# Threshold attention and a bilinear layer on one core: shorter reads of the turned weights, a changed front, stores by halves

## The chip, the core and the metric

The kernel runs on one core of a Trainium2 chip. The core has a matrix engine (PE, with its weight loads shown apart as PEld), a vector engine (DVE), a scalar engine (ACT), a general engine (POOL) and an engine that issues transfers (SP); 16 DMA engines move the data. Matrix products are written to PSUM, a small memory of banks; all else lies in SBUF, which has 128 partitions. The metric is the device time of the whole kernel in microseconds, as the median of several runs. One further execution is profiled, and all durations below are of that execution.

## The reference

```python
scores = (q @ k.T) / 8                          # 8 batches, 8 heads, 576 x 64 each
thresh = max(scores, axis=-1) - tau
scores = where(scores >= thresh, scores, -1e9)
attn = exp(scores - max(scores)); attn /= sum(attn) + 1e-9
x = (attn @ v) as (4608, 512)                   # heads side by side
out = ((x @ w_a) * (x @ w_b)) @ w_out           # 512 -> 1536 -> 512
```

q, k and v are 32-bit floats; the three weight matrices come as 64-bit floats and are turned into 32-bit ones on the chip.

## The kernel before

**Tiling.** Two heads make a pair, 32 pairs in all. The queries of a pair are cut into units of 128 (u = 0 to 3); the last 64 queries of two neighbouring pairs make a fifth unit (u = NT = 4). The list `units` gives their order: for the first four pairs first u = 0 and 1 of all of them, then the rest. The main loop (L1117) goes over slots g; slot g computes the scores of unit g and, woven in between, later stages of earlier units and parts of the second layer.

**A unit's way.** `scores` (L389) multiplies q and k on PE into two PSUM tiles, one a head. DVE takes the row maxima `mx` (L411) and subtracts the threshold's width to get `thr` (L412). `weigh` (L422): ACT scales the maximum to `bias` (L431) and takes Exp (L432) into `tw`; DVE multiplies it by the mask (L435) and sums. The weights are then turned. Up to unit 8 this is PE's work (`turn_pe`, L472: products with a diagonal of reciprocals). From unit 8 on, DVE transposes blocks of 32 x 32 (L502), four transfers of 144 KB write them to a scratch in DRAM (`swap<-tw`), and `turn_back` (L517) reads them back the other way round (`wT<-swap`), in two transfers of 288 KB. `product` (L538) multiplies them with v into `pv`. Two buffers `wT` stand for the two units of a product, so the reads of the next two units wait until a product is done.

**The weight matrices.** 36 pieces of 128 x 512. Each is loaded by SP (L271), split by ACT (L298 and L299), clamped by POOL (L305), given its sign by DVE (`convert_sign`, L311), shifted by DVE (`convert_shift`, L319) and added by POOL (`convert_add`, L324). The table `early` gives two pieces to each of the slots 0 to 3 and 10 to 14, and three to each of the slots 4 to 9; ACT's half is done in slot g and the rest, by `convert_rest(g, k)` for piece k, in slot g + 1. While that goes on (`state["wide"]`, slots 0 to 15), scores use 128 query columns a product. `advance` emits parts of the second layer on PE.

**The first four pairs.** `load_rows` (L193) loads all of q and k in rows, and PE transposes them (`prep_pe`, L368, by 96 rows at a time); DVE copies q out of PSUM (L383), ACT copies k. For all later pairs q and k come by `load` in blocks of 32 x 32 and are transposed by DVE (`prep`, L361, with the transposition at L365): q in two parts, `q0` (256 queries) and `q1` (320 queries), in two buffers that all pairs share.

**Order and pace.** Each engine works through its instructions in the order in which the program writes them (`keep_order`). Transfers go to SP's queue. Up to slot 36 `post` (L139) issues them where they are posted; after that (`state["paced"]`) they go into the list `bulk`, from which `pump` (L152) takes them one entry at a time. Each entry makes SP wait for the PE instruction that was last at that place; an entry of n elements is charged 320 x n / 36864 columns of PE's work (`passed`, L169) before the next is taken. Eight semaphores serve the transfers in turn: each transfer waits for the one eight before it.

**The second layer.** `ffn` works in blocks of 256 rows; its finished rows go to `pending` (`rows_out`, L1001), and `store` (L1011) posts them one slot later, 128 x 512 at a time (64 rows for the tail blocks).

Of the kernel before, what the change touches and what calls it, by code (L numbers as in the profile page):

```python
# [10 lines left out]
FP32 = mybir.dt.float32  # L11
# [43 lines left out]
def kernel(  # L55
# [38 lines left out]
    nc = tc.nc  # L94
    B, H, S, D = q.shape
    P = 128
# [3 lines left out]
    HP = H // 2  # L100
# [5 lines left out]
    R = 96  # L106
    NR = S // R
    SH = S // 2
# [84 lines left out]
    def load_rows(i, name, room, engine=nc.sync):  # L193

        b, hp = pairs[i]
        for j in range(2):
            rows = {"q": q, "k": k}[name][b, 2 * hp + j]
            engine.dma_start(room[:, :, j * D:(j + 1) * D], rows.rearrange("(n p) d -> p n d", p=R))
        loaded.setdefault(i, {})[name] = room

    def load_v(i, again=False):
# [106 lines left out]
    def convert_sign(n):  # L308
        if n in stages:
            low, hi = stages[n].bitcast(U32), raws.pop(n)[:, :, 1]  # L310
            nc.vector.scalar_tensor_tensor(out=low, in0=hi, scalar=0x80000000, in1=low,  # L311
                                           op0=ALU.bitwise_and, op1=ALU.bitwise_or)
            if n in taken:
                extra.append(taken.pop(n))

    def convert_shift(n):
        if n in stages:
            top = pieces[n][0].bitcast(U32)
            nc.vector.tensor_scalar(top, top, 3, None, op0=ALU.logical_shift_left)  # L319

    def convert_add(n):
        if n in stages:
            top, low = pieces[n][0].bitcast(I32), stages.pop(n).bitcast(I32)
            nc.gpsimd.tensor_tensor(top, top, low, op=ALU.add)  # L324
            state["added"] += 1
# [42 lines left out]
    def prep_pe(i, name):  # L368

        m = loaded[i][name]  # L370
        if name == "q":
            mT = first_sb[:, i * S:(i + 1) * S]
        else:
            mT = work.tile([P, S], FP32, tag="kT", bufs=HP, name="kT")
        tp = banks(SH, "tp")
        for c in range(2):
            for n in range(NR // 2):
                nc.tensor.transpose(tp[:, c, n * R:(n + 1) * R], m[:, c * (NR // 2) + n], ident[0:R, 0:R])
        prepared.setdefault(i, {})[name] = mT
        return mT, tp  # L380

    def prep_copy(mT, tp):
        nc.vector.tensor_copy(mT.rearrange("p (c k) -> p c k", c=2), tp)  # L383

    def columns():

        return P if state["wide"] else D

    def scores(i, u):  # L389
        qT, kT = prepared[i]["q" if i < HP else "q1" if u > 1 else "q0"], prepared[i]["k"]  # L390
        base = HALF if i >= HP and u > 1 else 0
        sc = [banks(SH, "sc") for _ in range(2)]
        wide = D if u == NT else columns()
        each = [(c, t, j) for c in range(2) for t in range(2 if wide == D else 1) for j in range(2)]
        if units.index((i, u)) < BY_HEAD:
            each.sort(key=lambda x: x[2])
        for c, t, j in each:
            r = slice(j * D, (j + 1) * D)
            if u < NT:
                m, o, q0 = j, t, u * P + t * D - base  # L400
            else:
                m, o, q0 = t, j ^ t, MAIN - base
                qT, kT = prepared[i + t]["q" if i < HP else "q1"], prepared[i + t]["k"]
            nc.tensor.matmul(sc[m][o * D:o * D + wide, c], qT[r, q0:q0 + wide],  # L404
                             kT[r, c * SH:(c + 1) * SH], start=True, stop=True)
        mx = small.tile([P, 2], FP32, tag="mx", name="mx")
        thr = small.tile([P, 2], FP32, tag="thr", name="thr")
        bias = small.tile([P, 2], FP32, tag="bias", name="bias")
        for j in range(2):
            c = slice(j, j + 1)  # L410
            nc.vector.tensor_reduce(mx[:, c], sc[j], axis=AX.XY, op=ALU.max)  # L411
        nc.vector.tensor_scalar(thr, mx, cut, None, op0=ALU.subtract)  # L412
        scored[i, u] = (sc, thr, bias, mx)
# [103 lines left out]
    def turn_back(i, u):  # L517

        key = "wT", i, min(u // 2, 1) if i >= HP else u // 2
        if u < NT or i < HP:  # L520
            flush(("tw", i, u))
            swap = swaps.pop((i, u)).rearrange("g p e -> p g e")
            turned[i, u] = turned_tile((i, u))
            for y in range(0, G, 2):
                post(key, (turned[i, u][:, y:y + 2].rearrange("p g s e -> p g (s e)"), swap[:, y:y + 2]))
        if i >= HP and u == (3 if i % 2 else NT):
            flush(("tw", i - i % 2, NT))
            swap = swaps[i - i % 2, NT].rearrange("g p e -> p g e")
# [482 lines left out]
    def store(n):  # L1011

        for _ in range(n):
            post("out", pending.pop(0))

    BLOCK_COLS = NF * 2 * HP * HALF + 2 * NF * DM

# [84 lines left out]
    nc.vector.tensor_tensor(cut, cut, big, op=ALU.add)  # L1102
    early = {}

    def convert_rest(g, k):

        for n in early.get(g - 1, [])[k:k + 1]:
            convert_sign(n)
            convert_shift(n)
            convert_add(n)  # L1110

    n = 0
    for g in range(NPIECES):
# [3 lines left out]
    for g in range(len(units) + PV_LAG):  # L1117
# [26 lines left out]
            running["owed"] -= NSLOT * P // 2  # L1144
        if g < 3:
            prep_copy(*prep_pe(g + 1, "q"))
        convert_rest(g, 0)
        if g == 0:
            for c in range(0, 2 * QUARTER - 2 * CW + 1, 2 * CW):
                extra.append(more_u32[:, c:c + 2 * CW].rearrange("p (f w) -> p f w", w=2))  # L1150
# [7 lines left out]
        load_weights(RAWS if g < 9 else 3, most=1)  # L1158
        if here:
            weigh(i, u)  # L1160
        for p in range(HP, NPR):
            for name, d in (("q0", 1), ("q1", 1)):
                if g == (second if name == "q1" else first)[p] - d - (name == "q1" and p % 2):
                    prep(p, name)
        if here and g < BY_PE:
# [33 lines left out]
        elif here:  # L1199
            reciprocal(i, u, nc.scalar if converting else nc.vector)  # L1200
            normalise(i, u)
        convert_rest(g, 1)
        if g <= BY_PE:
            advance(pace)
        convert_rest(g, 2)
        for n in early.get(g, [])[1:]:
            convert_first(n)
            convert_clamp(n)
        load_weights(RAWS if g < 9 else 3, most=1)
        for p in range(HP, NPR):  # L1210
            for name, d in (("q0", 3), ("k", 4), ("q1", 3)):
                if g == (second if name == "q1" else first)[p] - d - (name == "q1" and p % 2):
                    load(p, name)
        for p in range(1, NPR):
# [67 lines left out]
```

## Time and profile before

| | us |
|---|---|
| median of 3 runs | 1406.4 (1405.77, 1406.4, 1414.82) |
| the profiled execution | 1400.57 |
| its span | 1398.8 |
| PE busy | 1361.5 |
| DVE busy | 1013.9 |
| ACT busy | 680.8 |
| POOL busy | 492.8 |
| mean granted clock of PE | 0.998 of full speed |

The span runs from the first to the last instruction of the profiled execution; the 1.8 us that its time has more lie around it. The row of an instruction group tells when it starts, how long it lasts, on which engine and line, what it writes and reads, and in brackets how long its engine stood idle before it and what ended that. An instruction that is held up inside the engine, not by a semaphore, shows a longer duration instead.

### The profile page before, as it was taken

To read this page: it belongs to the slowest core of one execution; us is meant where nothing else is said; L and a number is where in the kernel's file an instruction comes from. 1 tells how busy PE (TensorE), PEld (TensorE's weight loads), DVE (VectorE), ACT (ScalarE), POOL (GpSimd) and SP (SyncE) were. 2 spreads that over 40 slices of the span, in tenths; PEclk is the share of its full clock that TensorE was granted. 3 is DMA by queue.
4 is the path that set the end of the run, shared out by engine and by line. 5 is a ranking of instruction groups with operands and counts; after the bars stand their busy time and mean duration, and the time that the engine had idled before them with its cause. 6 is when DMAs were issued, how large, how long until landed. Compare 5 with 4: busy or idle time off the path is not lost.

```text
span 1398.8 us, 76307 instructions
## 1 busy us (share of the span) xinstructions
PE 1361.5 (97%) x33836; PEld 1258.5 (90%) x33836; DVE 1013.9 (72%) x2205; ACT 680.8 (49%) x1248; POOL 492.8 (35%) x675
## 2 busy tenths in 40 slices
PE   7889999999999999999999999999999999999998
PEld 5677588999998799999999999998899998799998
DVE  6999877787777768786767776778777776745425
ACT  6977555545554555544454545454545455431110
POOL 2764543424150607060515142332515060708100
PEclk9999999999999999999999999999999999999999
DMA  9977876667666775676556775566656775550000
GB/s 211 241 212 223 204 206 173 174 170 187 174 154 168 190 192 155 176 190 160 143 143 160 186 180 159 136 190 169 181 130 161 199 190 154 137 146 19 4 19 18
DMA packets 327449, 223.21 MB, mean 160 GB/s; under 512 B 171600, under 2 KB 311632, under 8 KB 327120
## 3 DMA queue, kind: packets, MB, share of 16 engines
q1 hardware_dynamic: 323936, 216.95, 60.1%
q8 instruction: 266, 4.36, 1.3%
q10 hardware_dynamic: 3184, 1.38, 0.4%
q14 instruction: 63, 0.52, 0.1%
HBM read 128.58 MB, written 89.65 MB: 156 GB/s over the span
## 4 chain that ended last, share of the span: by engine, by line
PE 88%; DMA 5%; DVE 4%; SPq 2%; issue 1%; ACT 1%; ACTq 0%; DVEq 0%
PE pab L750 29%; PE po L920 22%; PE pab L854 18%; PE sc L404 9%; PE pv L546 9%; SPq L144 1%; DMA vm<-in_v_dram 1%; DMA wT<-swap 1%; DVE tw L435 1%; DVE mx L411 1%; DMA more_u<-in_moe_w_a_dram 1%; DVE low L311 0%; DMA more_u<-in_moe_w_b_dram 0%; DVE tw L502 0%; DMA sums_u<-in_k_dram 0%
## 5 line engine op out<-in xcount | busy, mean ns | idle before, releaser
L454 ACT ACTIVATE tw<-tw,rcp 128x576 f32<-128x576 f32 x272 | 196.1, 768 | 201.3 <-DVE rcp L448 201.3
L411 DVE TENSOR_REDUCE mx<-sc 128x1 f32<-128x576 f32 x288 | 204.6, 752 | 121.2 <-PE sc L404 120.9
L432 ACT ACTIVATE tw<-sc,bias,scalars 128x576 f32<-128x576 f32 x288 | 239.6, 832 | 10.4 <-DMA qT<-in_q_dram 0.4
L712 POOL TENSOR_TENSOR h<-h,u 128x512 f32<-128x512 f32 x28 | 35.2, 1277 | 590.4 <-DVE h L824 414.1
L435 DVE SCALAR_TENSOR_TENSOR tw<-sc,thr,tw 128x576 f32<-128x576 f32 x288 | 220.9, 797 | 12.3 <-ACT tw L432 11.9
L920 PE MATMUL po<-wo_sb,h 64*64 64x256 f32 (+1 forms) x3408 | 210.5, 367 | 0.0
L502 DVE STREAM_TRANSPOSE tw<-tw 128x576 f32<-128x576 f32 x272 | 194.4, 752 | 0.8 <-ACT tw L454 0.8
L920 PEld LDWEIGHTS po<-wo_sb,h 64*64 64x64 f32 x3408 | 169.8, 133 | 14.9
L404 PE MATMUL sc<-kT,qT 64*64 64x288 f32 x2016 | 170.3, 404 | 1.8 <-issue 0.9
L546 PE MATMUL pv<-wT,vm 64*64 64x128 f32 (+2 forms) x4896 | 164.0, 275 | 3.7 <-DMA vm<-in_v_dram 1.4
L546 PEld LDWEIGHTS pv<-wT,vm 64*64 64x64 f32 x4896 | 153.2, 133 | 12.0 <-issue 4.0
L920 PE MATMUL po<-sums_u,h 64*64 64x256 f32 x2448 | 156.6, 376 | 0.0
L883 POOL TENSOR_TENSOR h<-h 128x256 f32<-128x256 f32 x168 | 117.2, 731 | 110.9 <-PE po L920 106.1
L750 PE MATMUL pab<-xU,wb_sb 64*64 64x128 f32 x4352 | 137.8, 269 | 0.0
L920 PEld LDWEIGHTS po<-sums_u,h 64*64 64x64 f32 x2448 | 126.1, 133 | 12.3 <-DVE h L862 0.5
L750 PEld LDWEIGHTS pab<-xU,wb_sb 64*64 64x64 f32 x4352 | 133.3, 133 | 1.8 <-ACT h L806 0.5
L404 PEld LDWEIGHTS sc<-kT,qT 64*64 64x64 f32 x2016 | 108.8, 133 | 17.3 <-issue 4.9
L431 ACT ACTIVATE bias<-mx,scalars 128x1 f32<-128x1 f32 x288 | 82.7, 287 | 66.1 <-DVE mx L411 65.6
L553 ACT COPY xT<-pv 128x128 f32<-128x128 f32 (+1 forms) x68 | 17.6, 259 | 193.5 <-PE pv L546 193.5
L750 PE MATMUL pab<-xS,wa_sb 64*64 64x128 f32 x2176 | 108.5, 269 | 0.8 <-issue 0.8
L554 DVE COPY xT<-pv 64x128 f32<-64x128 f32 (+1 forms) x136 | 38.1, 280 | 80.5 <-PE pv L546 79.0
L535 ACT COPY kept<-po 128x512 f32<-128x512 f32 x65 | 34.8, 535 | 120.3 <-PE po L920 106.4
(163 smaller groups left out, 2468.7 us busy)
## 6 DMA issues: line engine op xcount, KB each, us to landing
wT<-swap SPq DMA_DIRECT2D x242, 288.0 KB, 3.8
swap<-tw SPq DMA_DIRECT2D x480, 144.0 KB, 3.1
vm<-in_v_dram SPq DMA_DIRECT2D x128, 72.0 KB, 2.6
swap<-tw SPq DMA_DIRECT2D x128, 72.0 KB, 2.9
kT<-in_k_dram SPq DMA_DIRECT2D x112, 72.0 KB, 3.2
wT<-swap SPq DMA_DIRECT2D x56, 144.0 KB, 3.6
out_dram<-kept SPq DMA_DIRECT2D x27, 256.0 KB, 3.7
qT<-in_q_dram SPq DMA_DIRECT2D x112, 40.0 KB, 2.8
```

Of the source, the lines that this page charges most:

```text
L404: nc.tensor.matmul(sc[m][o * D:o * D + wide, c], qT[r, q0:q0 + wide], kT[r, c * SH:(c + 1) * SH], start=True, stop=True)
L411: nc.vector.tensor_reduce(mx[:, c], sc[j], axis=AX.XY, op=ALU.max)
L431: nc.scalar.activation(bias[:, j:j + 1], mx[:, j:j + 1], AF.Copy, scale=e_nscale)
L432: nc.scalar.activation(wb[j], sb[j], AF.Exp, bias=bias[:, j:j + 1], scale=e_scale)
L435: nc.vector.scalar_tensor_tensor(out=wv, in0=sb[j], scalar=thr[:, j:j + 1], in1=wv, op0=ALU.is_ge, op1=ALU.mult, accum_out=sums[:, j:j + 1])
L454: nc.scalar.activation(w, w, AF.Copy, scale=rcp[:, j:j + 1])
L502: nc.vector.transpose(w, w)
L546: nc.tensor.matmul(pv[c * D:(c + 1) * D, y], vm[rows, s], wT[y](rows, s), start=(s == 0), stop=(s == NSLOT - 1))
L750: nc.tensor.matmul(out[c * D:(c + 1) * D, r, f * P:(f + 1) * P], w[g][k][rows, w0:w0 + D], moving[k][rows], start=(fresh and k == 0 and f ...
L854: nc.tensor.matmul(pab[c:c + columns(), r], w[rows, f // n, k, fs + c:fs + c + columns()], moving, start=(k == 0), stop=(k == H - 1))
L883: (nc.vector if state["over"] else nc.gpsimd).tensor_tensor(*a, **kw)
L920: nc.tensor.matmul(po[c * D:(c + 1) * D, r, y, cut], ht[rows, t0:t0 + D], other[rows, f, cut], start=(f == 0), stop=(f == NF // 2 - 1))
```

## The change

1. *Turned weights.* Once transfers are paced, `turn_back` posts four reads of 128 x 288 elements instead of two of 128 x 576.
2. *Maxima.* In the wide slots the two maxima of a unit are written to two free columns of the PSUM bank that holds half of the first head's scores, instead of to SBUF.
3. *Signs.* For the second and third piece of a slot `convert_rest` does both signs, then both shifts and adds. In slots up to 8 `advance` stands behind the signs and ahead of the shifts; before, it stood between the second piece and the third.
4. *Queries.* For the first four pairs only the first 288 queries are loaded in rows and transposed by PE. The `q1` part (320 queries, of which 32 are loaded twice) comes by `load` and `prep` as for later pairs: loaded in slots 5, 7, 10 and 12, transposed by DVE in slots 7, 9, 12 and 14, and used from u = 2 on.
5. *Stores.* Each store of 128 rows is posted as two of 64 rows.

```diff
     def load_rows(i, name, room, engine=nc.sync):
         b, hp = pairs[i]
+        n = NR // 2 if name == "q" else NR
         for j in range(2):
-            rows = {"q": q, "k": k}[name][b, 2 * hp + j]
-            engine.dma_start(room[:, :, j * D:(j + 1) * D], rows.rearrange("(n p) d -> p n d", p=R))
+            rows = {"q": q, "k": k}[name][b, 2 * hp + j, 0:n * R]
+            engine.dma_start(room[:, 0:n, j * D:(j + 1) * D], rows.rearrange("(n p) d -> p n d", p=R))
...
         if name == "q":
-            mT = first_sb[:, i * S:(i + 1) * S]
+            mT = first_sb[:, i * SH:(i + 1) * SH]
...
-        for c in range(2):
+        for c in range(1 if name == "q" else 2):
...
-        nc.vector.tensor_copy(mT.rearrange("p (c k) -> p c k", c=2), tp)
+        nc.vector.tensor_copy(mT, tp[:, 0])
...
     def scores(i, u):
-        qT, kT = prepared[i]["q" if i < HP else "q1" if u > 1 else "q0"], prepared[i]["k"]
-        base = HALF if i >= HP and u > 1 else 0
-        sc = [banks(SH, "sc") for _ in range(2)]
+        qT, kT = prepared[i]["q1" if u > 1 else "q" if i < HP else "q0"], prepared[i]["k"]
+        base = HALF if u > 1 else 0
+        whole_sc = [psum.tile([P, 2, 512], FP32, tag="banks", name="sc") for _ in range(2)]
+        sc = [x[:, :, 0:SH] for x in whole_sc]
...
-        mx = small.tile([P, 2], FP32, tag="mx", name="mx")
+        if state["wide"]:
+            mx = whole_sc[0][:, 0, SH:SH + 2]
+        else:
+            mx = small.tile([P, 2], FP32, tag="mx", name="mx")
...
-            for y in range(0, G, 2):
-                post(key, (turned[i, u][:, y:y + 2].rearrange("p g s e -> p g (s e)"), swap[:, y:y + 2]))
+            n = 1 if state["paced"] else 2
+            for y in range(0, G, n):
+                post(key, (turned[i, u][:, y:y + n].rearrange("p g s e -> p g (s e)"), swap[:, y:y + n]))
...
     def store(n):
         for _ in range(n):
-            post("out", pending.pop(0))
+            to, t = pending.pop(0)
+            for r in range(0, to.shape[0], D):
+                post(("out",), (to[r:r + D], t[r:r + D]))
...
-    def convert_rest(g, k):
-        for n in early.get(g - 1, [])[k:k + 1]:
-            convert_sign(n)
-            convert_shift(n)
-            convert_add(n)
+    def convert_rest(g, k, steps=(convert_sign, convert_shift, convert_add)):
+        for step in steps:
+            for n in early.get(g - 1, [])[k]:
+                step(n)
...
-        convert_rest(g, 0)
+        convert_rest(g, slice(0, 1))
...
-        for p in range(HP, NPR):
-            for name, d in (("q0", 1), ("q1", 1)):
+        for p in range(NPR):
+            for name, d in (("q0", 1), ("q1", 1))[p < HP:]:
...
-        convert_rest(g, 1)
+        convert_rest(g, slice(1, 3), (convert_sign,))
         if g <= BY_PE:
             advance(pace)
-        convert_rest(g, 2)
+        convert_rest(g, slice(1, 3), (convert_shift, convert_add))
...
-        for p in range(HP, NPR):
-            for name, d in (("q0", 3), ("k", 4), ("q1", 3)):
+        for p in range(NPR):
+            for name, d in (("q0", 3), ("k", 4), ("q1", 3))[2 * (p < HP):]:
```

More of the change, by code (lines that the diff above doesn't have):

```diff
@@ L402, in scores @@
                 m, o, q0 = t, j ^ t, MAIN - base
-                qT, kT = prepared[i + t]["q" if i < HP else "q1"], prepared[i + t]["k"]
+                qT, kT = prepared[i + t]["q1"], prepared[i + t]["k"]
             nc.tensor.matmul(sc[m][o * D:o * D + wide, c], qT[r, q0:q0 + wide],
                              kT[r, c * SH:(c + 1) * SH], start=True, stop=True)
-        mx = small.tile([P, 2], FP32, tag="mx", name="mx")
+        if state["wide"]:
+            mx = whole_sc[0][:, 0, SH:SH + 2]
+        else:
+            mx = small.tile([P, 2], FP32, tag="mx", name="mx")
         thr = small.tile([P, 2], FP32, tag="thr", name="thr")
```

## The prediction

> **What bounds the kernel now.** First the busy times, then the span cut into stretches (columns: length, then busy us of PE, PEld, DVE, ACT and POOL with instruction counts, granted clock, DMA share, GB/s):
>
> ```profile
> PE 1361.5 (97%) x33836; PEld 1258.5 (90%) x33836; DVE 1013.9 (72%) x2205; ACT 680.8 (49%) x1248; POOL 492.8 (35%) x675
> ...
> 30.00:35.00 5.00, 3.99 (x100) 3.30 (x100) 4.19 (x13) 4.61 (x11) 2.84 (x5) 1.00 1.14 227
> 60.00:70.00 10.00, 8.89 (x188) 7.92 (x186) 9.79 (x24) 9.15 (x20) 8.19 (x9) 1.00 1.01 259
> 500.00:750.00 250.00, 249.57 (x6498) 242.41 (x6494) 181.94 (x401) 120.43 (x218) 76.59 (x113) 1.00 0.62 162
> 1380.00:1398.80 18.80, 13.37 (x295) 13.12 (x287) 7.48 (x17) 1.76 (x3) 0.72 (x1) 0.92 0.11 30
> ```
>
> PE is idle 1398.8 - 1361.5 = 37.3 us in all. The stretches put 26.2 of it before 250 us, 5.3 between 250 and 1260, 0.4 to 1380 and 5.4 in the last 19. So after 250 us PE is the bound, and time is to be had or lost in the front, where pieces of weight are converted. There DVE is full from 50 to 130 us, ACT nearly so, and DMA is above 1.0 up to 70. Next, the instructions of that stage in order of time (start us, us):
>
> ```profile
> 57.22 0.58 DVE L412 TENSOR_SCALAR thr<-mx,scalars 128x2 f32<-128x2 f32 x1
> 57.16 0.61 POOL L305 TENSOR_SCALAR wa_sb<-wa_sb 128x512 f32<-128x512 f32 x1
> ...
> 54.35 1.50 DVE L319 TENSOR_SCALAR wa_sb<-wa_sb 128x512 uint32<-128x512 uint32 x1
> 53.92 1.66 POOL L324 TENSOR_TENSOR wb_sb<-wb_sb,more_u 128x512 int32<-128x512 int32 x1 [0.36 <-DVE wb_sb L319]
> ```
>
> A two-column `thr` that takes 0.23 us elsewhere takes 0.58 and ends with POOL's clamp; a shift of 0.42 takes 1.50 and ends just after POOL's add. DVE and POOL hold something in turn.
>
> **The maxima in PSUM.** `thr` (L412) reads them. DVE operations with an operand in PSUM keep their length beside POOL (L435: 0.80 to 0.82 us throughout), so I expect `thr` at 0.25. It was 0.58 to 0.65 at 25.9, 40.7, 47.5, 57.2, 66.2, 75.3 and 104.3 us: 0.35 each. Against it stand two waits that the change adds, as the built program's order shows. The second maximum (L411) now waits for the first, one bank being written twice: some 0.1 us in each of 16 wide slots (the two overlap by 0.07 today). And ACT's first `bias` (L431) now waits for `thr`, where it waited for the first maximum alone; behind it stand both Exps, and DVE's first multiply waits for the second `bias`. That moves ACT by the second maximum and `thr`, 0.7 + 0.2 = 0.9 us, where ACT is ready early. In the first slot that is on the path:
>
> ```profile
> 11.04 0.29 ACT L431 ACTIVATE bias<-mx,scalars 128x1 f32<-128x1 f32 x1 [3.17 <-DVE mx L411]
> ...
> 13.82 2.30 PE L404 MATMUL sc<-kT,first_u 64*128 64x288 f32 x8 [1.49 <-ACT kT L1169]
> ```
>
> PE waits for the kT copy behind the Exps: **+1.0 us** there. Elsewhere ACT is ready early at 16.9, 56.6, 74.6 and 103.6 us; there it has idle time of 1.2 to 2.7 us before its next work for PE: cost 0, or 4 x 0.9 = 3.6 if that cover fails.
>
> **288 queries at first.** Before the first scores PE runs 12 transposes in 2.15 us; three fewer save 0.5, and q's first transfer is half as long (PE waits for it until 5.04): between 0 and 1, I take 0.5. **-1.0 us.** DVE's copy of 0.75 us becomes about 0.45; PE waits for it at 18.64 (0.41): **-0.2**. At 27.14 PE waits 0.88 for xT, which stands behind a `thr` of 0.65: **-0.3**. The eight halved reads take 590 KB off the queue, 2.6 us at the 223 GB/s of 10 to 15 us. PE waits 1.4 us for vm between 31 and 40 us, but DVE is 84 to 98% busy there and is late next: with its two shorter `thr`, **-0.8**. At 46.83 ACT waits 0.72 for a weight: **-0.5**.
>
> The other 320 queries come back as 16 reads of 40 KB on SP after slots 5, 7, 10 and 12 (655 KB, 2.7 us at 240 GB/s; at the 43 ns a packet of a late window rich in small ones, 5120 packets on 16 engines are 14 us). Only the first two fall on a full DMA, and no engine waits over a microsecond for a weight after 48 us, so 0, up to +3. SP's later weight loads stand behind them; their cover is the two to three slots by which weights are ahead. They add four DVE transposes of 0.47 us (the row of qT, L365) in slots that DVE fills: +1.9 in all.
>
> **Signs ahead of shifts.** In the six slots with three pieces, the third shift hits the add that the second has just released: at 54.35, 63.38, 80.97, 91.92 and 101.40 us it takes 1.5 instead of 0.42, and one sign 1.66 instead of 0.68: 6.4 us if all that goes. But what DVE and POOL hold in turn adds up, in the slot from 57.16 to 66.20 (9.04 us), to three adds of 1.27, three clamps of 0.61, three signs of 0.68, three shifts of 0.42, 0.35 for sums and rcp: 9.3, or some 8.6 without their overlapping ends. Reordering can use the 0.4 left, not the 1.08. Ends 0 and -6.4; I take 4 slots of 0.4, **-1.6**.
>
> The Trainium skill ("SBUF — State Buffer", Who interferes with whom) says that DVE's second port pair is GpSimd's, an exclusive lock that whoever issues first holds for the whole instruction. By that the collisions move and do not vanish, and the rows agree; were it a mere delay of the later one, the sum would be by 4.8 us lower.
>
> Three-piece slots (46 to 103 us): `thr` -1.4, maxima +0.6, signs -1.6, two transposes +0.9: **-1.5**. Two-piece slots to 150 us: maxima +0.6 and transposes +0.9, of which PE's own work there hides most: **+0.3**.
>
> **Turned weights in four.** 242 reads of 288 KB become 484 of 144 KB:
>
> ```profile
> wT<-swap SPq DMA_DIRECT2D x242, 288.0 KB, 3.8
> ...
> wT<-swap SPq DMA_DIRECT2D x56, 144.0 KB, 3.6
> ...
> 1093.92 4.31 SPq L157 DMA_DIRECT2D wT<-swap  x6
> ```
>
> SP's issue takes 0.38 us whatever the size, so it gains 242 x 0.4 = 100 us of work over 147 slots, 0.7 a slot of 8.5 with about 10 issues. The pacing charges by elements (320 columns a quarter), so the last quarter is posted 320 columns, some 0.55 us, later and lands 0.2 sooner. Reads are issued right after the product that frees the buffer and end 6 us or more before the next one: those of the row above at 1098.2, used at 1104.34, the tightest, where PE waited 1.1 us (and its weight load 1.3). Elsewhere 2.5 us or more remain after landing. **0**, between -1 and +2. Stores in halves add some 34 issues; nobody waits for a store but a `kept` buffer (5.5 and 4.6 us of ACT, off the path): **0**. The last stores, of 64 rows, are as before.
>
> **Sum:** -1.0 + 1.0 - 0.2 - 0.3 - 0.8 - 0.5 - 1.5 + 0.3 = **-3.0 us**. The profiled execution took 1400.57 (span 1398.8 and 1.8 around it), so 1397.6; the median of the runs is 1406.4, so **1403.4** on that scale. The runs lie between 1405.77 and 1414.82; about 1% is what a measurement here tells from no change.
>
> **Rivals.**
> - *Every collision goes* (0.15): the lock is only a delay; signs give 6.4 instead of 1.6, DMA's 2.6 us come through whole: -3.0 - 4.8 - 1.3 = -9, 1397. For it: POOL idles 1.2 us twice a slot. Against: the 8.6 of 9.04.
> - *The bank is the new wait* (0.25), slower: ACT behind `thr` in the front's wide slots. ACT is busy 9.15 of 10 us at 60 to 70, so once its idle is below 0.9 a slot the delay stays. All four further early slots +3.6, signs 0 (+1.6), start only -0.5 (+0.5), transposes and maxima unhidden +1.2: -3.0 + 6.9 = +4, 1410.
> - *Quarters crowd SP's queue* (0.08), slower: each transfer waits for the eighth before it, and 8 transfers of 3.6 us give one per 0.45, which is SP's pace already. If half of the 60-odd products then wait 0.5 us, it is +15, 1418. The slack of 2.5 us speaks against. The Trainium skill ("DMA: Bandwidth & Descriptors", Rules for kernel authors) speaks for it: coalesce small transfers, halves of the partitions do not help.
> - *The front's gain is not passed on* (0.05): PE waits for another engine a slot later; 0, 1406.
>
> The forecast keeps 0.47, from -5.5 to +1. The range 1397 to 1411 leaves out half of the first rival, some of the second and the third: 0.2. Faster by over 1% (below 1392.3) 0.05; slower by over 1% (above 1420.5) 0.08; within 0.87.
>
> **What will show it.** `thr` at or below 0.3 us in the wide slots; `bias` waiting for `thr` at about 11 us; the second score of PE at 13.8 unchanged; shifts of 1.5 us rarer but signs longer; PE's idle before 250 us down from 26 to about 23; between 250 and 1260 still near 5. It is wrong if ACT's waits before `bias` move the slots of 9.0 us, if PE waits for wT more than twice, or if those slots fall below 8.5.

## The result and the profile after

The changed kernel takes 1421.7 us, median of 8 runs (1414.67 to 1428.08), against 1407.4 of the kernel before, median of 8 runs (1403.06 to 1414.82). The ratio is **1.0092, 95% interval 1.0066 to 1.0117**: about 13 us slower. The forecast was 1403.4 with a range of 1397 to 1411, so both sign and size were wrong.

The profiled execution took 1423.92 us, 23.3 more than that of before. About 9 of these are the executions themselves: before's profiled one (1400.57) lies 7 us under the median of its runs and under all eight of them, after's 2 us over its median. The traces tell where time goes; how much a change costs is read from the ratios.

First the busy times of the page, then stretches of the span (columns as in the prediction):

```profile
PE 1367.0 (96%) x33824; PEld 1257.6 (88%) x33824; DVE 1009.8 (71%) x2209; ACT 679.3 (48%) x1248; POOL 492.5 (35%) x675
```

```profile
30.00:35.00 5.00, 4.12 (x113) 3.36 (x109) 4.64 (x10) 4.93 (x12) 4.00 (x6) 1.00 1.16 232
60.00:70.00 10.00, 8.51 (x183) 7.82 (x180) 9.25 (x22) 8.81 (x20) 7.21 (x9) 1.00 1.01 228
500.00:750.00 250.00, 248.93 (x6480) 236.25 (x6474) 178.83 (x394) 121.59 (x218) 74.09 (x111) 1.00 0.65 167
750.00:1000.00 250.00, 241.23 (x6052) 228.36 (x6048) 178.50 (x393) 118.14 (x215) 85.56 (x127) 1.00 0.64 161
1000.00:1260.00 260.00, 255.11 (x6557) 234.53 (x6553) 189.36 (x419) 129.79 (x232) 87.12 (x133) 0.99 0.63 161
1404.00:1422.10 18.10, 12.17 (x273) 11.93 (x265) 6.89 (x16) 1.17 (x2) 0.72 (x1) 0.89 0.12 31
```

Length less PE busy is PE's idle time. Laid beside the same stretches of before:

| stretch, us | before | after |
|---|---|---|
| 0 to 250 | 26.2 | 30.3 |
| 250 to 750 | 2.5 | 4.5 |
| 750 to 1000 | 1.2 | 8.8 |
| 1000 to 1260 | 1.6 | 4.9 |
| 1260 to the end | 5.9 | 6.7 |
| whole span | 37.3 | 55.1 |

So 12.9 of the 17.8 us of new idle time lie between 250 and 1260 us, where the prediction had "still near 5": it is 18.2. PE's busy time grew by 5.5 us as well.

What stands there is one chain, seen best at its longest. The timeline of the changed kernel from 947 us, with SP's transfers, DVE's transpositions and PE's first product and scores after it (start, length, engine, line; in brackets the idle time before and what ended it):

```profile
947.51 2.43 SPq L157 DMA_DIRECT2D out_dram<-kept  x4
948.96 1.43 DVE L507 STREAM_TRANSPOSE tw<-tw 128x576 f32<-128x576 f32 x2
950.05 3.24 SPq L157 DMA_DIRECT2D swap<-tw  x4
953.39 5.52 SPq L157 DMA_DIRECT2D wT<-swap  x10
959.01 2.55 SPq L157 DMA_DIRECT2D swap<-tw  x4
961.43 0.45 PE L552 MATMUL pv<-wT,vm 64*64 64x160 f32 x2 [1.82 <-issue]
961.65 2.69 SPq L157 DMA_DIRECT2D kT<-in_k_dram  x4
962.62 2.53 PE L552 MATMUL pv<-wT,vm 64*64 64x160 f32 x67 [0.74 <-issue]
966.53 0.78 DVE L366 STREAM_TRANSPOSE kT<-kT 128x576 f32<-128x576 f32 x1 [6.59 <-DMA kT<-in_k_dram]
968.47 0.71 PE L406 MATMUL sc<-kT,qT 64*64 64x288 f32 x8 [2.30 <-DVE h L821]
```

The same place of the kernel before, some 14 us earlier:

```profile
932.97 0.84 SPq L157 DMA_DIRECT2D out_dram<-kept  x2
936.82 3.88 SPq L157 DMA_DIRECT2D wT<-swap  x6
938.84 1.43 DVE L502 STREAM_TRANSPOSE tw<-tw 128x576 f32<-128x576 f32 x2
940.98 2.24 SPq L157 DMA_DIRECT2D swap<-tw  x4
943.36 3.35 SPq L157 DMA_DIRECT2D kT<-in_k_dram  x4
949.73 0.77 DVE L365 STREAM_TRANSPOSE kT<-kT 128x576 f32<-128x576 f32 x1
```

Read SP's rows from top to bottom: in the changed kernel each begins where the one above ends. In the changed kernel DVE has turned a unit's blocks at 950.39 (948.96 + 1.43), but SP has issued their four writes only at 961.56, **11.2 us later**, since ten reads (5.52 us) and the four writes of the unit before stand ahead. In the kernel before it is 940.27 and 943.22, 3.0 us. Behind the writes come the four loads of k. DVE, which works in order, stands 6.59 us at the transposition of kT; an addition of the second layer (L821) and the copies of xT stand behind it, and PE's scores wait for them, 2.30 us after PE has lost 1.82 and 0.74 at the product. The profile names these two "issue"; in the trace the last reads of the turned weights land at 961.34 and 962.53, 0.09 us before PE goes on each time.

These waits in the whole trace (total us, times, longest), and the time that SP itself waited for DVE's turned blocks, the part of its spare time that is used as a measure below; after:

```profile
DVE kT L366 <- DMA kT<-in_k_dram: 24.7, 9, 6.6
...
SPq L157 <- DVE tw L507: 61.8, 25, 5.6
```

and before:

```profile
DVE kT L365 <- DMA kT<-in_k_dram: 2.1, 4, 0.8
...
SPq L157 <- DVE tw L502: 112.0, 54, 6.5
```

SP waited 112 us for this and now waits 62. All its pauses of over 0.15 us between the end of one transfer and the start of the next, from 320 to 1260 us, add up to 288 of the 940 us in the kernel before and to **135** in the changed one. The longest stretch without such a pause was 23.4 us (36 transfers); it is now 46.5 us (73 transfers). In such stretches a transfer follows the one before it by 0.63 us in the mean, not by 0.38. SP has more to issue (page, transfers: count, size, median us to landing):

```profile
wT<-swap SPq DMA_DIRECT2D x444, 144.0 KB, 3.1
wT<-swap SPq DMA_DIRECT2D x48, 288.0 KB, 4.2
```

They land 0.7 us sooner (3.1 against 3.8), and 194 more of them are issued. Whether the finer entries of the list, each with its own wait for PE, make SP late instead is one of the theories below.

### The profile page after: what moved, and what is told of

The parts are those of the page before. It is cut to its first block, busy times and chain, and to the rows that moved or that the text cites. A ratio compares the mean times of both kernels' runs of the same rounds, so it can differ in the third digit from the quotient of the medians.

```text
span 1422.1 us, 76827 instructions
## 1 busy us (share of the span) xinstructions
PE 1367.0 (96%) x33824; PEld 1257.6 (88%) x33824; DVE 1009.8 (71%) x2209; ACT 679.3 (48%) x1248; POOL 492.5 (35%) x675
## 4 chain that ended last, share of the span: by engine, by line
PE 86%; DVE 5%; DMA 4%; SPq 2%; issue 2%; ACT 1%; DVEq 0%; ACTq 0%
PE pab L756 29%; PE po L926 21%; PE pab L860 17%; PE sc L406 10%; PE pv L552 9%; SPq L144 1%; DMA kT<-in_k_dram 1%; DMA wT<-swap 1%; DVE sc L416 1%; SPq L157 1%; DVE tw L440 1%; DVE low L312 1%; PE tp L488 0%; DVE tw L507 0%; PE po L996 0%
## 5 line engine op out<-in xcount | busy, mean ns | idle before, releaser
L416 DVE TENSOR_REDUCE mx<-sc 128x1 f32<-128x576 f32 x256 | 181.8, 752 | 112.6 <-PE sc L406 112.2
L440 DVE SCALAR_TENSOR_TENSOR tw<-sc,thr,tw 128x576 f32<-128x576 f32 x288 | 221.0, 797 | 12.9 <-ACT tw L437 11.3
L406 PE MATMUL sc<-kT,qT 64*64 64x288 f32 (+1 forms) x2128 | 190.0, 405 | 10.6 <-DVE xT L560 3.2
L552 PE MATMUL pv<-wT,vm 64*64 64x128 f32 (+2 forms) x4896 | 168.4, 277 | 10.4 <-issue 4.4
L552 PEld LDWEIGHTS pv<-wT,vm 64*64 64x64 f32 x4896 | 156.1, 134 | 20.0 <-issue 10.4
L406 PEld LDWEIGHTS sc<-kT,qT 64*64 64x64 f32 (+1 forms) x2128 | 117.7, 134 | 33.0 <-issue 13.4
L756 PE MATMUL pab<-xS,wa_sb 64*64 64x128 f32 x2176 | 108.5, 269 | 0.1
L436 ACT ACTIVATE bias<-mx,scalars 128x1 f32<-128x1 f32 x256 | 73.4, 287 | 56.9 <-DVE mx L416 56.6
L756 PE MATMUL pab<-xT,wa_sb 64*64 64x128 f32 x1856 | 93.2, 269 | 0.2
```

What stands on the lines that cost most here:

```text
L436: nc.scalar.activation(bias[:, j:j + 1], mx[:, j:j + 1], AF.Copy, scale=e_nscale)
L440: nc.vector.scalar_tensor_tensor(out=wv, in0=sb[j], scalar=thr[:, j:j + 1], in1=wv, op0=ALU.is_ge, op1=ALU.mult, accum_out=sums[:, j:j + 1])
L552: nc.tensor.matmul(pv[c * D:(c + 1) * D, y], vm[rows, s], wT[y](rows, s), start=(s == 0), stop=(s == NSLOT - 1))
L756: nc.tensor.matmul(out[c * D:(c + 1) * D, r, f * P:(f + 1) * P], w[g][k][rows, w0:w0 + D], moving[k][rows], start=(fresh and k == 0 and f ...
```

## The experiments

Theories. **A**: the loss is SP's issuing; each further transfer takes some 0.48 us of SP, and where pairs begin SP is full, so that whatever stands behind is late. **B**: the front changes lose it. **C**: the stores in halves. **D**: the finer pacing, by which the last quarter is held back and every entry has a wait of its own. **E**: the reads' size, their landing, the data path, whoever issues them. Ratios are to the kernel before, run on the same chip in the same rounds.

### Which part of the change

The changed kernel with reads in two, all else changed:

```diff
-            n = 1 if state["paced"] else 2
-            for y in range(0, G, n):
+            for y in range(0, G, 2):
```

> The changed kernel with change 1 undone: a unit's turned weights come back in two reads of 288 KB again, all else as in the changed kernel. Theory A (SP's queue: each further transfer costs SP some 0.48 us of issue; with 218 more of them SP falls behind where pairs begin, the k loads are issued late, DVE stands at the transposition of kT and PE behind it): the loss goes, 0.996 to 1.002 of the kernel before; PE's idle time between 250 and 1260 us back at 5 to 8 us (16 to 18 in the changed kernel); DVE's waits for kT under 5 us in all (24.7). Theory B (the front lost it, in a way that only shows later): still 1.006 to 1.012. Theory C (the stores in halves): still 1.006 to 1.012.

Measured: 1.0029 (1.0008 to 1.0050); DVE's waits for kT 3.6 us, PE idle 9.2 us between 250 and 1260. Most of the loss goes, but time and idle time both stay a little over what A said (1.002 and 8 us).

The kernel before with the four reads alone:

> The kernel before with change 1 alone: four reads of 144 KB a unit. Theory A (SP's queue): the whole loss is here, 1.007 to 1.013, with DVE's waits for kT at 15 us or more in all and PE idle 12 us or more between 250 and 1260 us. Theories B and C (front, stores): 0.998 to 1.002.

Measured: **1.0090** (1.0062 to 1.0118), 12.7 us of 1408; DVE waits 15.1 us in 6 times for kT, PE is idle 12.6 us between 250 and 1260.

The three front changes alone:

> The kernel before with the three front changes alone (maxima in PSUM, signs ahead of shifts, 288 queries at first); reads of the turned weights in two, stores whole. The prediction's sum for these is -3.0 us, 0.998. Theory A: 0.996 to 1.001, with what the front gains up to 150 us partly given back between 150 and 200 us, where PE waits for wT. Theory B (the front lost it): 1.006 to 1.012.

Measured: 1.0013 (0.9991 to 1.0034), kT waits 0.3 us. B falls: most of the loss is in the four reads. But the front's -3.0 (0.998) is outside the interval too.

The stores alone:

> The kernel before with change 5 alone, the stores in halves of 64 rows: some 34 more transfers. Changed kernel without the four reads was at 1.0029, the front changes alone at 1.0013; by that the stores are worth 1.0016 or 2.3 us. Theory A (0.06 us of loss a transfer, as 12.7 us for 194 in the kernel with the four reads alone): 1.000 to 1.003. If stores cost nothing, as the prediction had it: 0.998 to 1.001.

Measured: 1.0028 (1.0012 to 1.0043), 3.9 us: not nothing, and more than 0.06 us for each of 34 transfers. The rows of SP say why (count, then shortest/median/longest ns). With halves:

```profile
L157 SPq DMA_DIRECT2D out_dram<-kept x52: 467/541/1916, 351.1 to 1245.0; - x52
```

and whole, in the kernel before:

```profile
L157 SPq DMA_DIRECT2D out_dram<-kept x28: 362/390/1096, 348.0 to 1231.3; - x28
```

A store of 64 rows takes SP 0.54 us, one of 128 rows 0.39: two halves are 1.08 us for 0.39. C holds for about 0.3 of the loss: 3.9 us of some 13. The parts, each measured alone, add up to more than the whole (12.7, 3.9 and 1.8 us for the front).

### Pacing, number or size

Two quarters in one entry: as many transfers as in the changed kernel, the entries and the charge of the kernel before.

```diff
-            for y in range(0, G, n):
-                post(key, (turned[...][:, y:y + n]..., swap[:, y:y + n]))
+            moves = [(turned[...][:, y:y + n]..., swap[:, y:y + n]) for y in range(0, G, n)]
+            for y in range(0, len(moves), len(moves) // 2):
+                post(key, *moves[y:y + len(moves) // 2])
```

> The changed kernel, but two reads of 144 KB are posted as one entry of the list: as many transfers and as many bytes as in the changed kernel, half the entries, half the waits for PE, and the charge of 640 columns taken at once as before. Theory A (the number of issues): no better than the changed kernel, 1.006 to 1.013 of the kernel before. Rival D (the finer pacing: the last quarter is held back 320 columns more, and each entry has a wait of its own): the loss goes, 0.996 to 1.003.

Measured: 1.0109 (1.0077 to 1.0141), kT waits 18.9 us. D falls.

The kernel before, with a transfer of 20 bytes behind each read of 288 KB:

```diff
-                post(key, (turned[...][:, y:y + 2]..., swap[:, y:y + 2]))
+                post(key, (turned[...][:, y:y + 2]..., swap[:, y:y + 2]), (tiny[0:1, 0:5], scalars[0:1, 0:5]))
```

> The kernel before, with a second transfer of 20 bytes put behind each read of 288 KB, in the same entry of the list and of no charge: 218 more transfers, as many as the four reads bring, and no bytes to speak of; the reads, their sizes and the pacing are those before. The tiny transfers' data is used by nothing. Theory A (the issue alone): as bad as the four reads, 1.006 to 1.013, DVE's waits for kT 12 us or more. Rival E (size and landing of the reads) and rival D (pacing): 0.998 to 1.002.

Measured: 1.0039 (1.0016 to 1.0062), kT waits 10.2 us in 6 times. Transfers without data cost 5.5 us, so the issue alone does cost time; but it is less than half of the four reads' 12.7, where A said as bad. Part of it is that a tiny transfer takes SP less:

```profile
L157 SPq DMA_DIRECT2D tiny<-scalars x194: 230/312/662, 311.5 to 1263.0; - x194
```

The 194 tiny ones add 66 us of issue (the durations of all of SP's transfers, 798.5 us before, are 864.6), the 194 quarters 113 (911.3). That is 0.6 of the load for 0.43 of the loss; whether the rest is that the loss grows faster than the load, or that the quarters cost elsewhere too, is open.

Twice the dose, of another kind: the writes of turned blocks in eight, the reads in two.

```diff
-                moves = [(to, of)]
+                moves = [(to[:, r:r + 2], of[:, r:r + 2]) for r in range(0, G, 2)]
```

> The kernel before with each write of the turned blocks cut in two, eight of 72 KB a unit where there were four of 144 KB, posted in the same entries at the same charge: some 430 more transfers, of another kind, and the reads in two. Theory A (what counts is the number that SP issues, whatever they carry): with twice the added transfers of the four reads, 1.015 to 1.035, DVE's waits for kT over 25 us. Rival E (the reads' own size): 0.998 to 1.003.

Measured: **1.0408** (1.0376 to 1.0439), 57 us. Its waits:

```profile
DVE kT L365 <- DMA kT<-in_k_dram: 52.8, 10, 7.4
...
SPq L157 <- DVE tw L502: 21.5, 24, 2.9
```

The reads are cut as before, so such a loss needs no smaller reads; the writes are smaller, so it does not speak against E's data path. 384 more transfers have eaten SP's spare time, 112 down to 21.5 us. The writes also stand in the way of the reads of the same unit, so this dose is not a clean double. SP's spare time, from the same row of one profiled execution of each, goes with the ratio in the kernels that add transfers to SP, apart from neighbours whose intervals overlap:

| kernel | SP's spare time, us | ratio |
|---|---|---|
| before | 112.0 | 1 |
| front alone | 108.5 | 1.0013 |
| stores in halves alone | 98.7 | 1.0028 |
| tiny transfers | 94.7 | 1.0039 |
| front and stores | 92.2 | 1.0029 |
| four reads alone | 71.5 | 1.0090 |
| quarters in one entry, front, stores | 68.6 | 1.0109 |
| the changed kernel | 61.8 | 1.0092 |
| writes in eight | 21.5 | 1.0408 |

### Is the late k the way?

The changed kernel, k on the list one slot earlier (`("k", 4)` to `("k", 5)`):

> The changed kernel with k of the later pairs put on the list one slot (some 8.5 us) earlier, on SP as before; four reads a unit, stores in halves, as many transfers in all. SP stays as late as in the changed kernel, but what is late no longer has DVE waiting for it. Theory A, and that the late k is the way by which SP's lateness reaches PE: DVE's waits for kT fall from 24.7 us to under 4, PE idle between 250 and 1260 us from 18 to under 10, 1.002 to 1.006 of the kernel before. If SP's lateness reaches PE mainly by the turned weights themselves, or if the transfers are late for another reason: 1.007 to 1.012.

Measured: 1.0113 (1.0094 to 1.0132). DVE waits for kT no more (0.0), and nothing is won. Its timeline at the same place:

```profile
956.69 1.43 DVE L507 STREAM_TRANSPOSE tw<-tw 128x576 f32<-128x576 f32 x2
959.18 2.70 SPq L157 DMA_DIRECT2D swap<-tw  x4
959.84 0.78 DVE L366 STREAM_TRANSPOSE kT<-kT 128x576 f32<-128x576 f32 x1
963.05 4.03 PE L552 MATMUL pv<-wT,vm 64*64 64x160 f32 x69 [3.80 <-DMA swap<-tw]
```

PE now stands 3.80 us at the product, for turned weights that stood behind k. PE's idle time between 250 and 1260 us stays at 16.4 us, where under 10 was forecast, and the time lies in the range set for the alternative. SP's lateness reaches PE by whichever transfer stands last; k was only one of those in the changed kernel's order.

The same edit on the kernel before:

> The kernel before with k put on the list one slot earlier, no other change. Its own waits for kT are 2.1 us in 4 times in the profiled execution, so there is little to gain: 0.996 to 1.000, DVE's waits for kT under 0.5 us. If the executions of the kernel before that take 1412 us are those in which SP is late, the longest ones go and the spread (1402.5 to 1414.8) narrows.

Measured: 1.0055 (1.0038 to 1.0072): a miss. kT waits are gone, but PE waits 8.7 us at the product after 140 us for turned weights (1.1 before), and the longest runs did not go (1412.47 to 1420.39). This kernel has SP's spare time of 115.2 us and loses all the same: the order of the transfers counts beside their number.

### Taking transfers off SP

k's loads issued by ACT, on the changed kernel and on the front changes alone:

```diff
-                post((name, i), *some)
+                if name == "k" and state["paced"]:
+                    nc.scalar.dma_start(*some[0])
+                else:
+                    post((name, i), *some)
```

> The changed kernel with one thing moved: once transfers are paced, the four loads of k of each pair are issued by ACT at the place where they were put on the list, and no longer by SP. As many transfers and bytes as in the changed kernel, 84 or so fewer on SP's queue (some 0.65 us each), and the loads that DVE waits for no longer stand behind the turned weights. Theory A (SP's queue is late): DVE's waits for kT fall from 24.7 us to under 2, PE's idle time between 250 and 1260 us from 18 to under 9, and the time comes to 0.997 to 1.004 of the kernel before. Rival E (the data path itself: more and smaller transfers land later, whoever issues them): 1.006 to 1.012, with waits for kT as long as before.

> The front changes alone (reads in two, stores whole) with the k loads of the paced part issued by ACT. Theory A: with SP's queue eased below that of the kernel before, the front's gain is no longer given back: 0.994 to 0.999, with PE idle under 5 us between 250 and 1260 us and no wait of DVE for kT. If the front's gain is lost for another reason: 0.999 to 1.003.

Measured: 1.0266 (1.0235 to 1.0297) and 1.0134 (1.0106 to 1.0161). kT waits are 0 in both, but ACT is no free issuer (timeline of the first):

```profile
967.00 8.31 ACTq L191 DMA_DIRECT2D kT<-in_k_dram  x4
975.35 0.59 ACT L869 COPY h<-pab 128x512 f32<-128x512 f32 x1 [7.97 <-DMA kT<-in_k_dram]
```

Four issues hold ACT for 8.31 us. The eight semaphores are shared with SP: the third of the four loads starts at 974.05, when a read of wT that SP had issued at 968.05 on the same semaphore has landed (974.03). Both forecasts were missed, and the experiment says nothing of A.

v's loads issued by POOL instead, on the changed kernel and on the kernel before:

```diff
+                if state["paced"]:
+                    for c in range(2):
+                        nc.gpsimd.dma_start(half[c * Q:(c + 1) * Q], rows[:, c])
+                    continue
```

> The changed kernel with one kind of transfer moved: once transfers are paced, the four loads of v of each later pair are issued by POOL where they were put on the list; 100 or so transfers fewer on SP, which keep to no semaphore turn with SP's if POOL's transfers have their own. Theory A (SP's queue): about half of what the four reads brought is taken off SP again, 1.003 to 1.006 of the kernel before, SP's lag behind DVE's turned blocks under 10 us at its longest (13.4 in the changed kernel). If SP's number of issues is not the cause: 1.008 to 1.012. If POOL's issuing holds up its own work: over 1.012, with PE waiting for POOL.

> The kernel before with v's loads of the paced part issued by POOL, nothing else. SP has 90 or so transfers fewer. Theory A: 0.995 to 1.000, as the executions in which SP is late go; if nothing is to be had from an easier SP: 0.999 to 1.002; if POOL's issuing holds up its work: above 1.002.

Measured: 1.0091 (1.0066 to 1.0117) and 1.0033 (1.0014 to 1.0053). A missed both, and the first lies where the number of issues is not the cause. But POOL's issuing has a price. In the kernel before with it, 6.6 us lie between the end of the last issue (1408.8) and the end of the span (1415.4), against 2.9 (1395.9 and 1398.8): the end of the program takes 3.7 of the 4.7 us. In the changed kernel with it the end takes 6.6 us for 3.5; without these 3.1 us it would be at 1.0069, still over A's 1.006, though SP's longest lag is under 10 us as forecast (9.9). So kernels with POOL as issuer are to be compared with each other. Two differ, once transfers are paced, in the four reads alone: v's loads and whole stores by POOL, all front changes, reads in four or in two.

```diff
+            if state["paced"]:
+                nc.gpsimd.dma_start(*pending.pop(0))
+                continue
```

> The changed kernel with v's loads and the stores (whole again, 128 rows) issued by POOL once transfers are paced: some 160 transfers fewer on SP, which leaves it with 70 or 80 more than in the kernel before; four reads a unit as in the changed kernel. Theory A: 0.999 to 1.004 of the kernel before, PE idle between 250 and 1260 us under 9 us, DVE's waits for kT under 6. If the number is not the cause: 1.007 to 1.012.

> The front changes alone, with v's loads and the stores of the paced part issued by POOL; reads in two. SP has 120 transfers fewer than in the kernel before. Theory A: 0.993 to 0.999; PE idle between 250 and 1260 us under 5 us, no half-clock windows. If nothing is to be had from an easier SP: 0.999 to 1.003.

Measured: **1.0068** (1.0043 to 1.0093) in four, **1.0065** (1.0043 to 1.0086) in two. With SP eased the four reads cost 0.0003, some 0.4 us (the means of the two kernels' runs differ by 0.7 us, with a standard error of 2.0), where they cost 12.7 us (8.7 to 16.6) on the kernel before. Waits of the one in four:

```profile
DVE kT L370 <- DMA kT<-in_k_dram: 7.8, 5, 2.2
...
SPq L157 <- DVE tw L511: 102.7, 42, 6.8
```

and of the one in two:

```profile
SPq L157 <- DVE tw L511: 152.8, 72, 6.8
```

With the same 444 reads of 144 KB as in the changed kernel, SP's spare time is back at 103 us. That answers E: while SP has room the quarters do no harm that these runs can tell. The absolute forecasts were missed (up to 1.004, and under 0.999), and so were those for PE's idle time between 250 and 1260 us: 10.9 and 12.6 us, for under 9 and under 5. In both kernels 8.9 us lie between the last issue and the end, 6.0 more than in the kernel before, which is some 0.0043 of each ratio. The other 0.0022 to 0.0025 were not traced.

The opposite direction, one read of 576 KB a unit (`n = G`), on the kernel before and on the front changes:

> The kernel before, changed in the opposite direction: once transfers are paced, a unit's turned weights come back in one read of 576 KB (128 rows of 4 x 288), where the kernel before has two and the changed kernel four; the charge of 1280 columns is taken at once. 96 transfers fewer on SP. Theory A (the number that SP issues): 0.994 to 0.999, no wait of DVE for kT, SP's lag under 8 us at its longest (9.3 before). If the number did not matter and the size of a read did: 1.001 to 1.006, with PE waiting for wT, as a read of 576 KB lands later.

> The three front changes with one read of 576 KB a unit; stores whole. Theory A: as the one read on the kernel before, and no worse than it: 0.994 to 1.000. The front changes alone were at 1.0013.

Measured: 1.0042 (1.0026 to 1.0058) and 1.0029 (1.0012 to 1.0046), both missed. SP's spare time rises to 138 and 140 us, DVE waits 3.6 and 1.8 us for kT, and yet they are slower, the first in the range set for the case that the size of a read matters. Why, the traces do not settle: such a read lands after 4.8 us (median), against 3.8, and SP waits 49.7 us (on the kernel before with one read) for writes of turned blocks to land, against 16.9, but no wait of PE between 250 and 1260 us names the turned weights. An SP with more room than before gains nothing. No version beat the kernel before.

### The front's terms

The front changes with the maxima in SBUF:

> The front changes alone, but the maxima written to SBUF as before: signs ahead of shifts and 288 queries at first are left. By the prediction's terms: the second slot then begins 1.0 us earlier than in the kernel with all three (no wait of ACT for thr); by slot 11 it is level with it or up to 1.4 us later (thr at 0.6 beside POOL again); between slots 11 and 16 it gives back 0.8 to 1.0 us less, as the pair of maxima takes 1.42 us and not 1.63. In the whole 0.996 to 1.002, not to be told from 1.0013.

Measured: 1.0004 (0.9990 to 1.0018). Its second slot begins 1.18 us earlier than with the maxima in PSUM (-1.08 against +0.10 us to the kernel before), as the prediction's term for the bank has it. At slot 11 it was expected level or up to 1.4 us later, but its maxima start at 98.8 us there, against 100.6 in the front alone and 99.6 in the mean of the ten executions described below (their standard deviation is 0.7): a miss, in one execution. That the maxima in PSUM gain anything in the sum is not shown. From slot 11 to 16 it takes 0.5 us less than the front alone and 0.8 less than the ten, about as expected.

## Why the prediction was wrong

**The step that failed: "Turned weights in four ... 0, between -1 and +2".** Alone it measures +12.7 us (8.7 to 16.6). Its sizes were near: landing falls (3.8 to 3.1 us), and SP gains some 100 us of issue (113, or 122 by 194 times 0.63). It counted 242 reads over 147 slots where only the 194 after slot 36 are cut, but that, too, is some 0.7 us a slot. Three things went wrong.

First, it spread SP's work evenly, "0.7 a slot of 8.5 with about 10 issues". SP's load is not even: from 928.1 to 971.4 us, where pairs begin, it issues 61 transfers at 0.71 us each, with one pause of 0.34 us, and what it cannot issue in time it carries along, 11.2 us of it.

Second, it looked at the reads alone. The price falls also on what stands behind them, the writes, k and q, whose users wait in order.

Third, it gave the reads a cover that they did not have. "End 6 us or more before the next one ... at 1098.2" is the end of their issue; in the trace of the kernel before the last of those reads lands at 1103.23, 1.1 us before the product at 1104.34, and another lands 1.6 us before its product. PE does not wait there; its one wait for `wT` at the product stands at 170.4 us:

```profile
PE pv L546 <- DMA wT<-swap: 1.1, 1, 1.1
```

In the changed kernel PE stands, between 250 and 1260 us, 7.6 us at scores that wait for DVE's late work, and 5.4 us at the product just until reads of turned weights land (two of these waits are the 1.82 and 0.74 above). With the four reads alone it is 9.4 us at the scores and none for the reads.

**"Stores in halves ... nobody waits for a store: 0"** fails in the same way, at +3.9 us (1.7 to 6.1): nobody waits for a store, but k waits behind it, and "0.38 us whatever the size" is not so for 64 rows (0.54), nor, in the kernel before already, for the loads of k (0.58).

**The rival "Quarters crowd SP's queue" (0.08) named the place** and nearly the time (1418). Its mechanism, each transfer waiting for the eighth before it, is not what the trace shows: SP's waits at L157 for a landed transfer are 1.1 us in the changed kernel and were 18.1 before. It is the issue itself; the time came near by another sum, which is luck. The rule from the Trainium skill cited there ("DMA: Bandwidth & Descriptors", Rules for kernel authors: coalesce) agrees with the four reads, the tiny transfers and the eight writes; the one read of 576 KB, 1.0042, speaks against following it further. The same page (Issuing engines are not separate DMA queues) says that another issuing engine only saves the time to initiate a transfer, usually small beside the transfer. It is small here, 0.38 to 0.55 us beside 3.1, and it decided.

**The front, point by point.** In the lines that answer to those of the prediction:

```profile
11.19 0.26 ACT L436 ACTIVATE bias<-sc,scalars 128x1 f32<-128x1 f32 x1 [4.37 <-DVE thr L417]
...
13.91 2.30 PE L406 MATMUL sc<-kT,first_u 64*128 64x288 f32 x8 [2.24 <-ACT kT L1176]
...
51.09 1.10 DVE L312 SCALAR_TENSOR_TENSOR low<-more_u,low 128x512 uint32<-128x512 uint32 x1
52.45 0.41 DVE L320 TENSOR_SCALAR wa_sb<-wa_sb 128x512 uint32<-128x512 uint32 x1
52.61 1.39 POOL L325 TENSOR_TENSOR wb_sb<-wb_sb,more_u 128x512 int32<-128x512 int32 x1 [0.97 <-DVE wb_sb L320]
55.20 0.61 POOL L306 TENSOR_SCALAR wa_sb<-wa_sb 128x512 f32<-128x512 f32 x1
55.27 0.22 DVE L417 TENSOR_SCALAR thr<-sc,scalars 128x2 f32<-128x2 f32 x1
```

- Start -1.0 and bank +1.0: right. The first slot begins 1.05 us earlier; ACT's `bias` waits for `thr`, and the second scores start at 13.91 (13.82 before).
- `thr` beside POOL: right, 0.22 us in every wide slot, also when it runs together with the clamp.
- Signs: the shift is 0.41 where it was 1.50, and a sign is 1.10 where it was 0.68: the collisions move, as the Trainium skill's exclusive lock ("SBUF — State Buffer", Who interferes with whom) has it. They also shrink: over all 36 pieces DVE's signs and shifts take 48.7 us before and 45.5 in the changed kernel (44.8 in the front alone). That is twice the 1.6 that the term took, between its ends of 0 and 6.4.
- The sum to 103 us was -3.3. For a steadier figure, the starts of the slots of ten profiled executions with these front changes were averaged, and of seven with the front of before (the two with an earlier k and the one with maxima in SBUF left out). At slot 11, near 103 us, they stand 4.6 us apart (standard error 0.8): right in sign, 1.3 low.
- **"Two-piece slots to 150 us +0.3, PE's own work hides most": wrong, +2.4.** At slot 17 the gap is 2.2 us (0.8). DVE is busy for 24.3 of the 25 us from 103 to 128 in the kernel before, so that what it gets to do is not hidden. The front changes alone at that place:

```profile
109.03 1.63 DVE L416 TENSOR_REDUCE sc<-sc 128x1 f32<-128x576 f32 x2
110.69 0.22 DVE L417 TENSOR_SCALAR thr<-sc,scalars 128x2 f32<-128x2 f32 x1
114.56 0.51 DVE L366 STREAM_TRANSPOSE qT<-qT 128x320 f32<-128x320 f32 x1
```

  The pair of maxima takes 1.63 us for 1.42, and two transpositions of 0.51 come in by slot 16. Over slots 11 to 15 that is 5 x 0.21 + 1.0, less the 1.4 by which five `thr` are shorter: 0.65. The larger rest of the 2.4 was not traced to rows.
- Between slots 18 and 24 PE waits for wT in both kernels, and the gap shrinks to 1.4 us (0.9). What is left of the front at 200 us is within what the ratio of the front alone allows, 1.0013, whose interval reaches down to -1.3 us.

**A sign of being wrong, named beforehand**, was "if PE waits for wT more than twice". It came true (4 times at L552), though two of the four, and most of the time, stand before 200 us, where the reads are in two as before.

**PE's busy time**, +5.5 us, had no step. A part is the clock, below; the rest is open.

## What to carry to other kernels

A queue that one engine issues has a capacity, and a mean over the kernel hides it: count the transfers of the busiest stretch, times the time from one issue to the next, against that stretch's length, and look at how late the queue already runs there. Then ask what stands behind the added transfers, not only whether these are needed in time; and take a read's end from its landing, not from the end of its issue. A transfer that nobody waits for is not free, and moving the one that is waited for only changes who waits next.

## What the runs showed of the hardware

**A short stall of PE can cost it the clock as well.** The stall at 1124 us of the changed kernel, in the timeline, and the granted clock there (after the busy times):

```profile
1124.57 4.35 PE L552 MATMUL pv<-wT,vm 64*64 64x160 f32 x69 [2.07 <-DMA swap<-tw]
```

```profile
1123.00:1127.00 4.00, 2.43 (x34) 2.42 (x38) 1.10 (x2) 0.00 (x0) 0.00 (x0) 0.70 0.71 183
1127.00:1131.00 4.00, 3.22 (x61) 2.56 (x55) 1.28 (x3) 0.35 (x2) 0.00 (x0) 0.87 0.50 88
```

The clock records of the trace show half the clock from 1124.6 for 3.41 us, which costs PE up to 1.7 us more than the 2.07 that it stood. Between 90 and 1380 us such stretches, of 3.41 or 6.83 us, add up to 0 in the kernel before, 3.4 us in the changed one, 17.1 with the four reads alone and 30.7 with the writes in eight, each beside a wait of PE of 2 us or more; other waits of 2.3 and 3.2 us in the changed kernel brought none. The Trainium skill ("TensorE: Matmul & The Clock Gate", Part 1) describes a free-running window of about 3.4 us after which an idle PE is put to half its clock; the lengths agree, but the window need not be idle as a whole: here a wait of 2.07 us sufficed.

**SP's issue time depends on the form of the transfer.** Medians: 0.31 us for 20 bytes, 0.38 for reads of 128 rows whether 144 or 288 KB, 0.39 for a store of 128 rows and 0.54 to 0.55 for one of 64. And one transfer in nine takes over 0.9 us, 1.4 in the mean, without a wait before it (141 of 1302 from 320 to 1260 us in the changed kernel, 105 of 1098 before): these 202 us are a quarter of the 805 us that SP does not pause there. What they are, no run shows.

**Transfers issued by ACT were held 8.31 us for four** by semaphores that they share with SP's; those issued by POOL were not, at 0.50 us each, but the program's end took 3.7 us more with v's loads on POOL and 6.0 with the stores too.
